# Block-sparse attention and soft MoE: a written task order for the attention stage, sampled values copied by either of two engines, and more early places for weights

## The chip, the cores and the metric

The kernel runs on 1 core of one Trainium2 chip. The metric is the device time of one execution in microseconds (us), as the median of several runs. The engines are TensorE (PE; its weight loads are shown apart as PEld), VectorE (DVE), ScalarE (ACT), GpSimd (POOL) and SyncE (SP), which only issues transfers here. Each engine takes its instructions in order.

## What is computed

Attention over 4 batches of 8 heads, 768 positions and 64 channels, in blocks of 32: a query block sees its neighbours, the first and last block, and three sampled blocks; the first and last query block see everything. Its output goes through a soft mixture of 8 experts with 4 slots each. All in float32.

```python
mask = np.abs(blk_i - blk_j) <= window
mask = mask | (blk_i == 0) | (blk_j == 0) | (blk_i == n_blocks - 1) | (blk_j == n_blocks - 1)
for qb in range(n_blocks):
    for kb in sampled_blocks[qb]:
        mask[qb * block:(qb + 1) * block, kb * block:(kb + 1) * block] = True
scores = np.where(mask, scale * q @ k.T, -1e9)
x = softmax(scores) @ v                      # rows of all heads side by side: 3072 x 512
logits = x @ phi                             # 3072 x 32 slots
slot_input = softmax(logits, axis=0).T @ x
h = np.maximum(slot_input[e] @ w1[e], 0.0)   # for each expert e: 4 x 512 @ 512 x 1024
slot_out[e] = h @ w2[e]
out = softmax(logits, axis=1) @ slot_out
```

## The kernel before

**Stages.** Attention runs for about 250 us, batch by batch (b = 0 to 3). Each batch has two "dense" items (the first and last query block against all keys: scores `sd`, products `avd`) and 11 "pair" items of two query blocks each. Then follows the expert part: first layer (`pf`, 128 matmuls), second layer (`pso`, 256 matmuls), and the combination with the output (`po`, `ob`).

**A pair item.** POOL copies the neighbouring and the two outer key blocks into a staging tile `kst` (`fixed`, L455 and L457); ACT or POOL adds the three sampled ones, whose block numbers stand in registers (`sampled_`, L463 and L465). The registers are filled by loads from the tables `sreg` and `vreg` (`block_numbers`, L362), three numbers a load. The query block is loaded by SP (`load_q`, L330) and scaled by ACT or POOL (L498, L500). PE forms the scores `s` (`qk`, L536: 32 matmul passes of a tile 64 rows by 32 columns). DVE takes the negated maximum `nm` (L551), ACT the exponentials `p` (L556), DVE the 32 x 32 transposes `ptt` (L563). POOL copies the sampled values to `vrs` (`stage_v`, L481, three copies of 128x260 a query block). Then PE multiplies with the values into `av` (`av_heads`, L628), DVE divides by the sums into `x` (L621 to L623), and PE transposes `x` (`mxt`, L823).

**Tilings of TensorE.** `av_heads` writes three widths one after another: the two outer blocks 128 columns wide, two neighbours 64 wide, the rest (other neighbour and the sampled blocks) 32 wide. Scores are 32 wide, transposes use the full 128 x 128 array, logits `ml` and slot sums `ms` 128 rows by 32 columns.

**Groups.** Four `x` tiles make a group: logits `ml`, their running maximum, `md`, `lt` and `ms` (`plan_group`).

**What sets the order.** Every piece of work is a task with a key, dependences, buffers that it takes, and one or more engines with a cost. `Plan.run` is a list scheduler: at each step it starts the task that can start earliest, with the key (shifted by the table `OFF`) deciding among near ones, and picks the engine for tasks with two. It emits the instructions in that order; where PE would stand idle it adds matmuls on the identity (`warm`, L396, tile `st`). Weight loads during attention are "paced": they are tied to a PE instruction of about their planned time.

**Weights.** The two layers are cut into 64 halves of 512 KB. 11 have places of their own, 15 take the room of keys, values and dense probabilities that are done with, 15 (`LORD`) the room of the attention's staging tiles when that stage ends; the other 23 wait for a half that has been used (`done_w`, `next_w`). All are issued by SP at L231.

Of the kernel before, what the change touches and what calls it, by code (L numbers as in the profile page):

```python
# [57 lines left out]
LORD = [0, 1, 2, 3, 4, 5, -1, -2, -3, -4, 6, 7, 8, -5, -6]  # L58
LCOLS = [slice(c, c + LC) for c in range(0, WP, LC)]
# [3 lines left out]
SWITCH = 0.095  # L63
BACK = {"PE": 0.17, "DVE": -0.07, "ACT": -0.1, "POOL": -0.06, "SP": 0.0, "NONE": 0.0}
OFF = {"acc": 4.15, "av": 2.35, "av1": 4.1, "av2": -5, "avo": -4.9, "avo1": -5, "ce": 5, "cm": -2.05,
       "cn": 0.65, "dav": 3.7, "davo": -3.85, "dexp": 1.8, "do": 2.9, "dqk": 0.05, "dt": 4.55, "dtop": 0.85,
       "dtrn": -4.55, "exp": 2.7, "fix": 4.3, "ldq": 3.55, "lexp": -1.45, "lg": -0.55, "lo": -2.85, "lp": -5,
       "lt": 5, "ltop": -5, "qk": 0.85, "scl": 3.05, "smp": 3.9, "sum": -3.1, "top": -4.8, "trn": 0.2,
       "vst": 4.7, "xt": -2.8, "xto": -1}
# [5 lines left out]
class Task:  # L75
    def __init__(self, f, opts, deps, key, acq, byte, pre, pace, kind, mode, ni):
        self.pace, self.kind, self.mode, self.ni = pace, kind, mode, ni
        self.f, self.opts, self.deps, self.key = f, opts, [d for d in deps if d], key
        self.acq, self.byte, self.pre = list(acq), byte, pre
        self.start = self.fin = self.eng = None  # L80


class Plan:
# [6 lines left out]
    def add(self, f, opts, deps, key, acq=(), byte=0, pre=None, pace=False, kind=None, mode=None, ni=0):  # L90
        t = Task(f, opts if isinstance(opts, list) else [opts], deps, key + OFF.get(kind, 0.0), acq, byte, pre, pace,
                 kind, mode, ni)
        self.tasks.append(t)
        return t

    def run(self):
        tasks = self.tasks
# [3 lines left out]
        left = {t: len(t.deps) for t in tasks}  # L101
        ready = {t: 0.0 for t in tasks}
        out = {t: [] for t in tasks}
        for t in tasks:
            for d in t.deps:
                out[d].append(t)
# [3 lines left out]
        queue = {p: sorted([t for t in tasks if any(q == p for q, _ in t.acq)], key=lambda t: t.key)  # L110
                 for p in self.pools if p not in self.free}
        gives = {t: [] for t in tasks}
        spans, open_ = [], {}
        avail = [t for t in tasks if not t.deps]
        order = []
        while avail:
            cand = []
            for t in avail:
                r, ok, k = ready[t], True, {}
                for p, _ in t.acq:  # L120
                    i = (nxt[p] + k.get(p, 0)) % self.pools[p]
                    k[p] = k.get(p, 0) + 1
                    if (p in queue and queue[p][0] is not t) or held[p][i]:
                        ok = False
                        break
                    r = max(r, slot[p][i])
                if ok:
                    if t.pace:
                        r = max(r, paced)

                    st, e, d = min(((max(r, at[e]), e, d) for e, d in t.opts), key=lambda z: (z[0], z[0] + z[2]))
                    if e == "PE" and t.mode and t.mode[0] != mode:
                        d += SWITCH
                    cand.append((st, t.key, st + d, t, e, d))
            assert cand, [(t.key, t.opts) for t in avail][:8]
            soon = min(c[:3] for c in cand)
            eng = min(cand, key=lambda c: c[:3])[4]
            st, _, en, t, e, d = min((c for c in cand if c[4] == eng and c[0] <= soon[0] + 0.05), key=lambda c: c[1:3])
            avail.remove(t)
            if e == "PE":  # L140
                mode = t.mode[-1] if t.mode else None
            t.start, t.eng, at[e] = st, e, en + BACK[e] + (0.11 if t.kind in ("qk", "dqk") else 0.0)
# [9 lines left out]
            else:  # L152
                t.fin = en
            order.append(t)
            for p in {p for p, _ in t.acq}:
                if p in queue:
                    queue[p].pop(0)
            for p, users in t.acq:
                i = nxt[p]
                nxt[p] = (i + 1) % self.pools[p]  # L160
                held[p][i] = set(users)
                for u in users:
                    gives[u].append((p, i))
                spans.append([p, i, st, 1e9])
                open_[p, i] = spans[-1]
# [5 lines left out]
            for o in out[t]:  # L171
                left[o] -= 1
                ready[o] = max(ready[o], t.fin + LAG[e])
                if not left[o]:
                    avail.append(o)
        assert len(order) == len(tasks), len(tasks) - len(order)

        todo = {e: [t for t in order if t.eng == e and t.pre] for e in at}
        pe_end = 0.0
        pe = []  # L180
        for t in order:
# [4 lines left out]
            if t.eng == "PE":  # L186

                if (t.start > self.fill[0].fin and t.start - pe_end > 0.45
# [15 lines left out]
def attn_moe_kernel(ctx, tc, qT, kT, vfull, vtab, sampled, phi, w1, w2, out):  # L204
# [968 lines left out]
    with tc.manual_schedule(engines={E_.SP}):  # L1173
        plan.run()
# [280 lines left out]
```

## Time and profile before

| | |
|---|---|
| median of 3 runs | 311.37 us (309.15 to 311.98) |
| span of the profiled execution | 305.7 us |
| PE busy | 277.5 us (91%), 7161 matmuls and 7161 weight loads |
| DVE, ACT, POOL busy | 215.4, 166.1, 178.9 us |
| moved by DMA | 63.61 MB, mean 208 GB/s |
| granted clock of PE | 1.00 nearly everywhere (mean 0.984) |

The span runs from the first to the last instruction of the profiled execution; the run times also hold what lies around it. A row of a timeline merges neighbouring instructions of one kind: its second number runs to the end of the last one. Ends of matmuls are modelled, so how long a piece of PE work really took is best read from its start to the start of the next piece. "issue" as the end of an idle time means that the profile shows nothing that was waited for.

### The profile page before, as it was taken

Reading aid. Unit: us, or ns where it says so; the run is one execution under the profiler, and the core shown is the slowest. Engines: PE = TensorE matmul, PEld = TensorE weight load, DVE = VectorE, ACT = ScalarE, POOL = GpSimd, SP = SyncE. Lnnn points to the kernel's source line nnn. Section 1 sums busy time; section 2 is a strip of 40 time slices with the busy share of each in tenths; the row PEclk is TensorE's granted clock in tenths of the full one; section 3 lists DMA queues with packets and bytes.
Section 4 is the critical chain, followed back from the end, with each engine's and each line's share of the span. In section 5 each row is a group of like instructions: output and inputs, shape, how many; then the busy total and the mean of one; then the engine's idle time right before and its main releaser. Section 6 shows DMA issues by size and latency. Waiting matters only on the chain.

```text
span 305.7 us, 17569 instructions
## 1 busy us (share of the span) xinstructions
PE 277.5 (91%) x7161; PEld 193.2 (63%) x7161; DVE 215.4 (70%) x494; ACT 166.1 (54%) x515; POOL 178.9 (59%) x501
## 2 busy tenths in 40 slices
PE   7688999799999999999999999999897999999950
PEld 6248775476687767767777767867665763355640
DVE  4698878458998779988988879998676545012360
ACT  0875847453667877446689654695641142102450
POOL 2669589927855899684599977579753504000000
PEclk9899999999999999999999999999999999999995
DMA  7946677630166672035376320778979998999998
GB/s 238 401 122 174 184 203 219 171 109 3 38 181 186 192 188 78 5 90 142 115 206 192 118 74 21 206 194 232 232 215 317 412 404 286 401 409 407 369 314 274
DMA packets 31634, 63.61 MB, mean 208 GB/s; under 512 B 5313, under 2 KB 18754, under 8 KB 31554
## 3 DMA queue, kind: packets, MB, share of 16 engines
q1 hardware_dynamic: 31408, 62.37, 64.1%
q8 instruction: 56, 0.92, 1.2%
q14 instruction: 24, 0.20, 0.2%
q10 hardware_dynamic: 146, 0.13, 0.1%
HBM read 56.19 MB, written 6.29 MB: 204 GB/s over the span
## 4 chain that ended last, share of the span: by engine, by line
PE 76%; DMA 7%; issue 4%; ACT 3%; DVE 2%; POOL 1%; SPq 1%; POOLq 1%; ACTq 1%
PE av L628 30%; PE s L536 11%; PE avd L628 7%; PE pso L1261 5%; PE pf L1253 5%; PE mxt L823 4%; DMA q<-in_qT_dram 4%; PE sd L732 4%; PE ml L859 2%; DMA v<-in_vfull_dram 2%; PE ms L909 2%; PE po L1357 1%; DMA out_dram<-ob 1%; POOLq L362 1%; PE st L396 1%
## 5 line engine op out<-in xcount | busy, mean ns | idle before, releaser
L481 POOL COPY vrs<-v 128x260 f32 x264 | 94.7, 405 | 25.4 <-PE av L628 17.5
L556 ACT ACTIVATE p<-s,nm 128x256 f32<-128x256 f32 x176 | 72.3, 483 | 13.9 <-DVE nm L551 12.5
L628 PE MATMUL av<-v,ptt 64*64 64x130 f32 (+2 forms) x1728 | 75.8, 285 | 1.4 <-issue 1.3
L628 PEld LDWEIGHTS av<-v,ptt 64*64 64x64 f32 (+2 forms) x1728 | 50.1, 131 | 25.7 <-issue 18.7
L563 DVE STREAM_TRANSPOSE ptt<-p 128x512 f32<-128x512 f32 x88 | 57.3, 688 | 4.5 <-ACT p L556 3.8
L551 DVE TENSOR_REDUCE nm<-s 128x2 f32<-128x512 f32 x88 | 54.9, 680 | 4.0 <-PE s L536 3.8
L536 PE MATMUL s<-kst,q 64*32 64x256 f32 x1408 | 51.9, 385 | 6.4 <-POOL kst L465 3.0
L457 POOL COPY kst<-ktile 128x384 f32<-128x384 f32 x88 | 43.1, 506 | 15.4 <-PE s L536 14.6
L628 PE MATMUL av<-vrs,ptt 64*32 64x130 f32 x2112 | 46.9, 275 | 3.8 <-issue 3.7
L463 ACT ACTIVATE kst<-ktile 128x128 f32 x177 | 40.9, 310 | 11.7 <-PE s L536 10.4
L536 PEld LDWEIGHTS s<-kst,q 64*32 64x32 f32 x1408 | 30.5, 107 | 18.9 <-POOL kst L465 4.9
L628 PEld LDWEIGHTS av<-vrs,ptt 64*32 64x32 f32 x2112 | 35.8, 105 | 6.2 <-issue 5.7
L374 ACT COPY xT<-mxt 128x512 f32<-128x512 f32 (+1 forms) x25 | 14.1, 564 | 32.4 <-PE mxt L823 32.3
L628 PE MATMUL avd<-v,ptd 64*64 64x130 f32 x768 | 22.8, 271 | 1.5 <-DVE x L623 1.4
L628 PEld LDWEIGHTS avd<-v,ptd 64*64 64x64 f32 x768 | 21.6, 132 | 3.2 <-issue 1.6
L465 POOL COPY kst<-ktile 128x128 f32 x87 | 21.8, 293 | 0.5 <-issue 0.5
L621 DVE TENSOR_SCALAR rs<-av 128x8 f32<-128x8 f32 (+2 forms) x28 | 4.3, 155 | 23.7 <-PE av L628 23.7
L500 POOL TENSOR_SCALAR q<-q 128x256 f32<-128x256 f32 x23 | 9.3, 406 | 19.0 <-DMA q<-in_qT_dram 15.7
L732 PE MATMUL sd<-ktile,q 64*32 64x384 f32 x256 | 18.4, 510 | 0.9 <-ACT p L556 0.5
L498 ACT ACTIVATE q<-q 128x256 f32<-128x256 f32 x25 | 10.4, 425 | 15.3 <-DMA q<-in_qT_dram 15.2
L763 ACT ACTIVATE pd<-sd,nb 128x384 f32<-128x384 f32 x32 | 16.6, 580 | 3.5 <-DVE nb L758 3.1
L750 DVE TENSOR_REDUCE nm<-sd 128x1 f32<-128x384 f32 x32 | 16.2, 545 | 2.7 <-PE sd L732 2.7
(122 smaller groups left out, 290.1 us busy)
## 6 DMA issues: line engine op xcount, KB each, us to landing
w<-in_w_dram SPq DMA_DIRECT2D x20, 512.0 KB, 8.7
v<-in_w_dram SPq DMA_DIRECT2D x12, 512.0 KB, 10.5
q<-in_qT_dram SPq DMA_DIRECT2D x47, 128.0 KB, 2.7
w<-in_w_dram SPq DMA_DIRECT2D x44, 128.0 KB, 3.4
out_dram<-ob SPq DMA_DIRECT2D x22, 256.0 KB, 3.3
ktile<-in_kT_dram SPq DMA_DIRECT2D x48, 96.0 KB, 2.9
v<-in_w_dram SPq DMA_DIRECT2D x24, 128.0 KB, 4.4
kw<-in_w_dram SPq DMA_DIRECT2D x6, 512.0 KB, 8.7
```

What stands on the lines that cost most here:

```text
L457: POOL.tensor_copy(out=st[:, :, w:w + 96], in_=kv[:, :, (i - 1) * BLK:(i + 2) * BLK])
L463: ACT.activation(out=st[:, :, o:o + BLK], in_=src, func=AF.Copy, scale=1.0)
L465: POOL.tensor_copy(out=st[:, :, o:o + BLK], in_=src)
L481: POOL.tensor_copy(out=st[:, :, j:j + 1, :], in_=vf[:, :, ds(t.vals[j], 1), :])
L536: PE.matmul(u.s[r][32 * p:32 * p + 32, j, :], lhsT=u.q[s_, p, j, :], rhs=kd[j][0][s_, p, :], start=True, stop=True)
L551: DVE.tensor_reduce(out=u.nm[r], in_=u.s[r], axis=AX.X, op=ALU.max, negate=True)
L556: ACT.activation(out=u.p[r][:, j, :], in_=u.s[r][:, j, :], func=AF.Exp, bias=u.nm[r][:, j:j + 1], scale=1.0)
L563: DVE.transpose(out=T.pt[r][:, :, 2 * w:2 * w + 2, :].rearrange("p k j q -> p j k q"), in_=u.p[r].rearrange("p j (k q) -> p j k q", k=8))
L628: PE.matmul(av[:, r * 2 * D1:(r + 1) * 2 * D1].rearrange("p (a d) -> p a d", a=2), lhsT=lhsT, rhs=rhs, start=start, stop=stop)
L732: PE.matmul(u.s[r][k][32 * p:32 * p + 32, :], lhsT=T.dq.q[s_, p, j, :], rhs=kt[s_, p, 384 * k:384 * (k + 1)], start=True, stop=True)
L750: DVE.tensor_reduce(out=u.nm[r][:, k:k + 1], in_=u.s[r][k], axis=AX.X, op=ALU.max, negate=True)
L763: ACT.activation(out=u.p[r][k], in_=u.s[r][k], func=AF.Exp, bias=u.nb[r], scale=1.0)
```

## The change

1. `OFF`, the keys and the list scheduler no longer set the order: a table `ORDER` of 1291 task numbers does, for all engines; a `+` at a number takes the second engine of that task. The planned times that remain serve the pacing and how far ahead registers are loaded. The idle matmuls of `warm` inside the attention are no longer made.
2. `av_heads` can run its widths upwards (32, 64, 128) when the work ahead left the array 32 wide (`up`).
3. Sampled values may be copied by ACT (`stage_v`). Staging tiles are assigned when the task runs, not when it is planned.
4. Block numbers of the two query blocks of a pair are loaded together, six a load, once for each engine that uses them.
5. Transposes of two `x` tiles form one task.
6. Some two-input DVE operations on 1 or 2 columns become one-input ones (`nb`, `nmx`, `ssum`), and the subtraction and the product of the second softmax move to POOL (`c_low`, `c_share`).
7. Four more weight halves get a place: two in buffers of `ptt` and one in two buffers of `x` (asked for at the scores of the last item but one, `qks[N - 2]`), one in two buffers of `xT`.
8. `pf` takes other PSUM banks, since `pc` and `ph` are made first.

```diff
+ORDER = """
+0 21 4 5 1 6 7 9 8 37 2 14 3 10 16 12 38 13 22 15 11 17 82 23 65 20 29 25 18 24 33 34 35 26 36 63 30 27 78 28 39 79+
...
+""".split()
...
-        while avail:
...
+        for word in ORDER:
+            t = self.tasks[int(word.rstrip("+"))]
+            e, d = t.opts[word.count("+")]
...
             if e == "PE":
+                t.up = t.turn and t.mode[0] != mode and t.mode[-1] == mode
...
-                if (t.start > self.fill[0].fin and t.start - pe_end > 0.45
-                        and sum(p == "s" and a < t.start and z > pe_end for p, _, a, z in spans) < SB):
-                    self.fill[1](int((t.start - pe_end - 0.15) / 0.28))
...
+    def block_numbers(b, t, i, eng, most):
+        j = (i - 1) // 2
+        key = b, most, j, eng
+        if key not in both:
+            _, both[key] = nc.values_load_multi_w_load_instructions(
+                t[0:1, 2 * j + 1:2 * j + 3, :], engines=[{"ACT": E_.Activation, "POOL": E_.Pool}[eng]], min_val=0, max_val=most,
...
             for j in range(NR):
-                POOL.tensor_copy(out=st[:, :, j:j + 1, :], in_=vf[:, :, ds(t.vals[j], 1), :])
+                o, src = st[:, :, j:j + 1, :], vf[:, :, ds(t.vals[j], 1), :]
+                if t.eng == "ACT":
+                    ACT.activation(out=o, in_=src, func=AF.Copy, scale=1.0)
+                else:
+                    POOL.tensor_copy(out=o, in_=src)
...
-        for n in range(NR + 1):
+        for n in ((1, 2, 3, 0) if up else range(NR + 1)):
...
+        todo = low + mid + wide if up else wide + mid + low
...
-                DVE.tensor_tensor(out=u.nb[r], in0=nm[:, 0:1], in1=nm[:, 1:2], op=ALU.min)
+                DVE.tensor_reduce(out=u.nb[r], in_=nm, axis=AX.X, op=ALU.min)
...
+            t_t = add(turns, ("PE", 0.44 if len(both) == 1 else 0.85), sum([z[1].out for z in both], []), n + 2, kind="xt", mode="F", ni=8 * len(both),
+                      acq=[("pt", z[4]) for z in both] + [("xT", z[5]) for z in both])
...
+    for j in range(NPT):
+        add(lambda t, m=m + j: load_w(m, turned), ("SP", 0.47), [qks[N - 2]], N + j / 10, acq=[("ptt", end_use)], byte=4 * WP * P,
+            kind="lw")
...
+    add(lambda t, m=m + NPT: load_halves(m, "x", XB), ("SP", 0.94), [qks[N - 2]], N + 0.2, acq=[("x", end_use)] * 2, byte=4 * WP * P,
+        kind="lx")
...
+    wpool.append(None)
+    load_halves(len(wpool) - 1, "xT", XTB)
...
+    psF.tile([P, 4, P], F32, tag="po", name="pc", bufs=3)
+    ph = psF.tile([P, 8, NS], F32, tag="f1", name="ph", bufs=1)
     pf = [psF.tile([P, 512], F32, tag="pf", name=f"pf{hf}", bufs=2) for hf in range(2)]
```

On PE, in batch 0, around the second pass of transposes before: scores of two pair items, one tile's transposes, and a product with its three widths downwards (the first number of a size is the width in columns; a row stands for so many equal matmuls).

```order
L536 MATMUL s<-kst_95,q_97 32x256 x8
L536 MATMUL s<-kst_96,q_97 32x256 x8
L823 MATMUL mxt<-ident,x 128x128 x4
L628 MATMUL av<-v_68,ptt 128x130 x4
L628 MATMUL av<-v_68,ptt 64x130 x8
L628 MATMUL av<-v_68,ptt 32x130 x8
L628 MATMUL av<-vrs_103,ptt 32x130 x2
```

The end of the product that follows the same scores now, and what comes after it.

```order
L671 MATMUL av<-vrs_102,ptt 32x130 x2
L671 MATMUL av<-vrs_101,ptt 32x130 x2
L671 MATMUL av<-v_68,ptt 32x130 x8
L671 MATMUL av<-v_68,ptt 64x130 x8
L671 MATMUL av<-v_68,ptt 128x130 x4
L882 MATMUL mxt<-ident,x 128x128 x8
L671 MATMUL av<-v_68,ptt 128x130 x4
L671 MATMUL av<-v_68,ptt 64x130 x8
```

The product behind the scores begins 32 wide, as the scores are, and ends 128 wide; two tiles are transposed together, and the next product runs downwards from 128.

Counted over all of PE's rows up to the second layer of transposes for the row sums (`mr`), the array's tiling changes 184 times before and 154 times now; `st` has 24 matmuls before and 13 now.

On ACT, in batch 0, exponentials `p` and sampled keys `kst` before (an `ISA` row computes an address from a register):

```order
L362 TENSOR_LOAD sreg
L556 ACTIVATE p<-s,nm 128x256 x2
L362 TENSOR_LOAD sreg
L463 ISA
L463 ACTIVATE kst_95<-ktile 128x4x32
```

and now, where the loads from `vreg` and the copies to `vrs` stand between them:

```order
L394 TENSOR_LOAD vreg
L599 ACTIVATE p<-s,nm 128x256 x3
L394 TENSOR_LOAD vreg
L522 ISA
L522 ACTIVATE vrs_103<-v_68 128x2x130
```

ACT now holds register loads ahead of its exponentials as before, and the copies of values behind them.

On SP, the last paced weight pieces (32 rows each) and the first late halves (128 rows) before:

```order
L231 DMA v_68<-in_w_dram 32x1024 x14
L231 DMA ptd<-in_w_dram 32x1024 x12
L231 DMA kw<-in_w_dram 128x1024 x3
L231 DMA w_7108<-in_w_dram 128x1024
L231 DMA w_7110<-in_w_dram 128x1024
```

and now:

```order
L258 DMA kw<-in_w_dram 128x1024
L258 DMA w_7241<-in_w_dram 128x1024
L258 DMA w_7244<-in_w_dram 128x1024
L258 DMA kw<-in_w_dram 128x1024
L258 DMA v_68<-in_w_dram 32x1024 x2
L1184 DMA w_7336<-in_w_dram 128x512
L1184 DMA w_7337<-in_w_dram 128x512
L258 DMA w_7608<-in_w_dram 128x1024
```

The three halves in buffers of `ptt` and `x` (`w_7241`, `w_7244`, and `w_7336` with `w_7337`) stand ahead of the first half that takes the room of a staging tile (`w_7608`). Behind the 15 `LORD` halves comes the fourth; 19 halves wait for used ones, before 23.

Over the whole program POOL's copies to `vrs` go from 264 to 168 and ACT's from 0 to 96; sampled keys on POOL from 87 to 150, on ACT from 177 to 114; query scalings on POOL from 23 to 35, on ACT from 25 to 13; `xT` copies on ACT from 23 to 13, on DVE from 0 to 10; register loads on POOL from 117 to 76, on ACT from 59 to 58.

## Rows read from the trace of the kernel before

**Rows 1.** The page: busy time, share and instructions; DMA queue of instructions, packets and MB.
```profile
PE 277.5 (91%) x7161; PEld 193.2 (63%) x7161; DVE 215.4 (70%) x494; ACT 166.1 (54%) x515; POOL 178.9 (59%) x501
...
q8 instruction: 56, 0.92, 1.2%
```

**Rows 2.** Windows: stretch, length, busy us (instructions) by engine, clock, DMA share, GB/s.
```profile
44.00:61.00 17.00, 14.03 (x392) 8.74 (x388) 10.65 (x20) 11.53 (x36) 16.68 (x49) 1.00 0.70 192
61.00:203.00 142.00, 139.06 (x4271) 103.89 (x4276) 123.83 (x272) 93.81 (x300) 104.53 (x296) 1.00 0.43 121
203.00:252.00 49.00, 44.48 (x1129) 32.22 (x1131) 31.86 (x84) 22.33 (x73) 25.77 (x70) 1.00 0.92 296
160.00:170.00 10.00, 10.00 (x370) 7.99 (x372) 8.02 (x17) 7.97 (x26) 9.87 (x29) 1.00 0.67 194
```

**Rows 3.** Timeline of PE, 44 to 61 us: start, length, instructions, idle before.
```profile
45.84 1.33 PE L536 MATMUL s<-kst,q 64*32 64x256 f32 x31
...
49.19 0.66 PE L823 MATMUL mxt<-ident,x 128*128 128x128 f32 x4
49.77 1.71 PE L628 MATMUL av<-v,ptt 64*128 64x130 f32 x40
...
52.13 1.71 PE L628 MATMUL av<-v,ptt 64*128 64x130 f32 x40
...
54.41 0.62 PE L536 MATMUL s<-kst,q 64*32 64x256 f32 x6
...
59.73 0.66 PE L823 MATMUL mxt<-ident,x 128*128 128x128 f32 x4
```

**Rows 4.** Timeline of PE, 83 to 98 us.
```profile
88.52 1.96 PE L536 MATMUL s<-kst,q 64*32 64x256 f32 x64
90.41 0.65 PE L823 MATMUL mxt<-ident,x 128*128 128x128 f32 x4
90.99 1.71 PE L628 MATMUL av<-v,ptt 64*128 64x130 f32 x40
...
93.18 1.51 PE L536 MATMUL s<-kst,q 64*32 64x256 f32 x32
```

**Rows 5.** Timelines of ACT (44 to 61 us) and of SP's issues (30 to 60 us).
```profile
56.56 0.42 ACT L498 ACTIVATE q<-q 128x256 f32<-128x256 f32 x1 [4.03 <-DMA q<-in_qT_dram]
...
45.51 5.79 SPq L354 DMA_DIRECT2D v<-in_vfull_dram  x10
...
52.42 0.35 SPq L330 DMA_DIRECT2D q<-in_qT_dram  x1
```

**Rows 6.** Timeline of PE, 200 to 246 us.
```profile
231.63 0.88 PE L628 MATMUL av<-vrs,ptt 64*32 64x130 f32 x41
234.57 0.42 PE L628 MATMUL av<-vrs,ptt 64*32 64x130 f32 x7 [2.06 <-issue]
```

**Rows 7.** Waits: who waited for what, us in total, times, longest.
```profile
PE av L628 <- issue: 5.0, 7, 2.1
```

**Rows 8.** Instructions of line 362: duration ns min/median/max, first and last start.
```profile
L362 POOLq TENSOR_LOAD <-vreg x88: 721/728/751, 14.8 to 228.8; - x88
L362 ACTq TENSOR_LOAD <-sreg x59: 692/702/889, 2.2 to 219.0; - x59
```

**Rows 9.** Groups by line and shape: busy us, mean ns of one, idle before.
```profile
L481 POOL COPY vrs<-v 128x260 f32 x264 | 94.7, 405 | 25.4 <-PE av L628 17.5 <-PE s L536 2.2 <-DMA q<-in_qT_dram 1.9
...
L498 ACT ACTIVATE q<-q 128x256 f32<-128x256 f32 x25 | 10.4, 425 | 15.3 <-DMA q<-in_qT_dram 15.2
```

**Rows 10.** Late weights: SP's issues, a window, landing on the page, the chain.
```profile
252.83 6.07 SPq L231 DMA_DIRECT2D w<-in_w_dram  x9
...
275.34 1.68 SPq L231 DMA_DIRECT2D w<-in_w_dram  x2
...
252.00:256.00 4.00, 4.00 (x40) 1.30 (x36) 3.70 (x15) 1.21 (x3) 2.28 (x3) 1.00 0.76 232
...
w<-in_w_dram SPq DMA_DIRECT2D x20, 512.0 KB, 8.7
...
287.32 1.86 PE pso L1261 x32
```

More of the change, by code (lines that the diff above doesn't have):

```diff
@@ L62 @@
 HEAD = -4096
[L63 to L69, printed above, removed]
+SWITCH = 0.13
+FETCH, BORDER = 4.05, 192
+BACK = {"PE": 0.03, "DVE": -0.07, "ACT": -0.1, "POOL": -0.06, "SP": 0.0, "NONE": 0.0}
+ORDER = """
[47 rows of a table added]
+""".split()
 E_ = mybir.EngineType
@@ L100, in run @@
         mode = None
[L101 to L104, printed above, removed]
+        count, border, entered = 0, BORDER, -100.0
+        ready = {t: 0.0 for t in self.tasks}
+        out = {t: [] for t in self.tasks}
+        for t in self.tasks:
             for d in t.deps:
@@ new lines, in schedule @@
+        gives = {t: [] for t in self.tasks}
+        spans, open_, order = [], {}, []
+        for word in ORDER:
+            t = self.tasks[int(word.rstrip("+"))]
+            e, d = t.opts[word.count("+")]
+            st = max(ready[t], at[e], paced if t.pace else 0.0)
+            for p, users in t.acq:
+                i = nxt[p]
+                assert not held[p][i]
+                nxt[p] = (i + 1) % self.pools[p]
+                st = max(st, slot[p][i])
+                held[p][i] = set(users)
+                for u in users:
+                    gives[u].append((p, i))
+                open_[p, i] = [p, i, st, 1e9]
+                spans.append(open_[p, i])
+            if e == "PE":
+                t.up = t.turn and t.mode[0] != mode and t.mode[-1] == mode
+                if t.mode and t.mode[-1 if t.up else 0] != mode:
+                    d += SWITCH
+                mode = t.mode[0 if t.up else -1] if t.mode else None
+                n = t.ni + 2
+                while border < count + n:
+                    b = st + d * (border - count) / n
+                    wait = max(0.0, entered + FETCH - b)
+                    d += wait
+                    entered = b + wait
+                    border += 256
+                count += n
+            t.start, t.eng, at[e] = st, e, st + d + BACK[e]
@@ L152, in run @@
             else:
-                t.fin = en
+                t.fin = st + d
             order.append(t)
[L155 to L165, printed above, removed]
             for p, i in gives[t]:
@@ L359, in load_v @@
         return i
-    def block_numbers(t, i, eng, most):
-        _, vals = nc.values_load_multi_w_load_instructions(
-            t[0:1, i, :], engines=[{"ACT": E_.Activation, "POOL": E_.Pool}[eng]], min_val=0, max_val=most,
-            skip_runtime_bounds_check_because="block numbers lie in range by the definition of the input")
-        return vals
+    both = {}
+    def block_numbers(b, t, i, eng, most):
[4 more added lines that the diff above has]
+                t[0:1, 2 * j + 1:2 * j + 3, :], engines=[{"ACT": E_.Activation, "POOL": E_.Pool}[eng]], min_val=0, max_val=most,
+                skip_runtime_bounds_check_because="block numbers lie in range by the definition of the input")
+        o = (i - 2 * j - 1) * NR
+        return both[key][o:o + NR]
     def place(b, t):
@@ L916, in acc @@
                     continue
-                if gi:
+                if gi and o is ssum:
+                    DVE.tensor_scalar(out=o, in0=o, scalar1=st.al, scalar2=i, op0=ALU.mult, op1=ALU.add)
+                elif gi:
                     DVE.scalar_tensor_tensor(out=o, in0=o, scalar=st.al, in1=i, op0=ALU.mult, op1=ALU.add)
@@ L1082, in f_diff @@
     def f_diff(t):
-        fin.row = pw.tile([1, P], F32, tag="x", name="row", bufs=XB)
+        fin.row = phis[0:1].rearrange("p c s -> p (c s)")
         fin.top = pw.tile([1, NS], F32, tag="top", name="top", bufs=1)
@@ L1171, in attn_moe_kernel @@
     ms.__enter__()
-    plan.fill = max(qks.items())[1], lambda n: warm(None, n)
-    with tc.manual_schedule(engines={E_.SP}):
-        plan.run()
+    late = tc.manual_schedule(engines={E_.SP})
+    late.__enter__()
+    plan.run()
     warm(None, 1)
```

254 lines of the change are left out of this document (142 added, 112 removed), and 46 rows, old and new, of the table ORDER.

## Prediction

> **What bounds the kernel now.** I read the page first: PE is busy 277.5 of 305.7 us, and no other engine passes 71% [rows 1]. PE is therefore the engine whose time has to shrink, either because its work becomes less or because it waits less. Next I read PE by windows, to see where it waits. From 44 to 61 us it is idle for 17.00 - 14.03 = 2.97 us, from 61 to 203 us for 2.94 us in 142, from 203 to 252 us for 4.52 us in 49 [rows 2]. Idle time is not all: an instruction that is held also looks long, so I then measured pieces from start to start in PE's timeline. A double piece of scores (64 matmuls) takes 90.41 - 88.52 = 1.89 us, a tile's transposes 90.99 - 90.41 = 0.58, a product of 88 matmuls that is followed by scores 93.18 - 90.99 = 2.19 [rows 4]. Against these prices, the scores at 45.84 take 3.35 us and those at 54.41 take 5.32 [rows 3]: 1.46 + 3.43 = 4.9 us lost, most of what the window shows as idle being in it.
>
> What ended the longer of these two waits? ACT stood for 4.03 us until 56.56, waiting for a query block that it was to scale [rows 5]; its exponentials lay behind, and with them the score buffers that PE needs. That block was issued by SP at 52.42, behind ten value pieces that kept SP for 5.79 us from 45.51 on [rows 5]. At the same time POOL is busy 16.68 of 17.00 us [rows 2]. In the last stretch the longest wait is another: 2.06 us at 234.57, inside a product whose inputs were all there ("issue") [rows 6]; seven such waits of PE sum to 5.0 us [rows 7].
>
> **The change part by part.**
>
> *Fewer tilings.* The array changes its tiling 184 times before and 154 times now, 30 less. A product followed by another product takes 52.13 - 49.77 = 2.36 us [rows 3], and one followed by scores, which stay 32 wide, 2.19 [rows 4]: one change costs 0.17 us. The upward order (32 to 64 to 128) is in no row; the same two borders lie in it, so I charge it the same. 30 x 0.17 = 5.1 us at most, and nothing where PE would have waited anyway (a stretch with gaps swallows it). I take 0.15 a change: **-4.5 us**. The 11 matmuls of `st` that go filled idle time; they cost and gain nothing, since what covered them is the wait itself.
>
> *The stretch from 44 to 61 us.* Lost are 4.9 us. The new order puts 35 of 48 query scalings on POOL, 23 before, so a late block holds ACT's exponentials less often, and POOL is freed of 96 copies to `vrs` at 94.7 / 264 = 0.36 us each [rows 9], 34 us, against 63 more sampled keys, shorter copies of 128 instead of 260 elements, so at most 63 x 0.36 = 23 us. SP still puts runs of value pieces between query blocks. Bounds 0 and 4.9; I take **-3.5**, nearer to the top because both causes are eased.
>
> *61 to 203 us.* Idle are 2.94 us [rows 2], spread over many short waits; bounds 0 and 2.9; half or a little more is what a new order may find: **-2**.
>
> *203 to 252 us.* Idle are 4.52 us [rows 2]. The wait of 2.06 [rows 6] is no wait for data, so reordering moves it rather than removing it. Bounds 0 and 4.5; **-2**.
>
> *Copies on ACT.* A copy of 128x260 on ACT is not in the trace; the nearest is the scaling of 128x256 at 0.425 us [rows 9]. 96 of them make 41 us, less 63 sampled keys, 10 `xT` copies and 12 scalings that leave, so ACT, busy 54%, ends below 65%: it does not become the bound. But its order is fixed, and three copies in a row (1.3 us) ahead of an exponential delay the transposes and the product behind it. Nothing is lost if the exponential's product lies more than 1.3 us off, and 32 x 1.3 = 41 us if each of the 32 groups is on the path. PE's idle in the calm middle, 2% [rows 2], says that most waits have slack; I charge one and a half groups, 2 us.
>
> *Register loads.* Three numbers take 0.702 us on ACT's sequencer and 0.728 on POOL's, whatever lies around [rows 8]. Six numbers are in no row: between 0.7 (the load counts) and 1.4 (each number counts). There are 117 + 59 = 176 loads before and 76 + 58 = 134 now. If the load counts, 42 loads of 0.7 us go, 30 us over two sequencers; if each number counts, 528 numbers become 804 and 276 x 0.24 = 66 us come. Today these run ahead while the engine works off earlier instructions. I take them at no cost, the cover being those earlier copies; without it up to 0.7 us stand before each of ACT's 58. The Trainium skill ("Runtime: NRT & Kernel Launch", Instruction fetch mechanics) speaks against this edit: it gives about 200 ns a register even in bulk. By that, six numbers would take 1.2 us, near my upper end; the trace's 0.70 for three agrees with it, and the sum by it would be that of the slower rival below, as far as the cover fails.
>
> *The rest.* The two-input DVE operations, the second softmax on POOL and the pairs of block copies lie on engines that PE does not wait for: nothing, as long as DVE keeps its gaps (123.83 busy of 142 us in the middle [rows 2]); if these are gone, the ten `xT` copies come on top of it, at most 6 us. Other banks for `pf`: -0.2.
>
> *Weights.* An earlier end of the attention helps only if the weights follow. Late halves are issued back to back; SP waits once until 252.83 for a used half, and the window behind it moves 232 GB/s at a share of 0.76, about 1 us lost [rows 10]. The last two halves leave SP at 275.34 to 277.0, land about 8.7 us later (285.7), and are used near the end of the piece that runs from 287.32 to 289.18: 2 to 3 us of slack [rows 10]. The four new places close the hole (+1 us), and three halves, 1.5 MB, are asked for before the attention ends. The rest of the late loads hang on staging tiles that come free earlier when attention ends earlier. So I charge nothing.
>
> **Sum.** -4.5 - 3.5 - 2 - 2 + 2 - 0.2 = -10.2 us. The profiled span of 305.7 becomes 295.5. The runs' median lies 311.37 - 305.7 = 5.7 us above that span, which I keep: **301 us**. With the terms' own bounds for likely cases, 296 to 305.
>
> **The rivals.**
>
> *Slower: ACT becomes the step that PE waits for.* Place: register loads and value copies between exponentials of one item. Per group 1.3 us of copies and up to 1.4 us of load, 2.7 us. Gains of 12.2 us (the sum without its 2 us of cost) are eaten when 5 of 32 groups stand on the path with their full price; 3 us more, seven groups in all (18.9), make it slower, 311.4 - 12.2 + 18.9 = **318**. For it: ACT is busy 7.97 of 10 us already at 160 to 170 [rows 2]. Against it: its exponentials today share that room with 177 sampled-key copies, 63 of which leave.
>
> *The instruction stream bounds PE.* 2 x 7161 instructions come in 56 blocks [rows 1], 256 each. From 160 to 170 us PE takes 742 instructions, 2.9 blocks, without a gap [rows 2], one in 3.45 us; the 5.0 us of "issue" [rows 7] come where dense products meet a saturated DMA. If the denser order doubles them: 301 + 5.0 = **306**. The Trainium skill (same page and section) calls crossing a block mostly hidden; by it this rival would not exist, and the 2.06 us of [rows 6] disagree.
>
> *The weights cap it.* If paced pieces and staging tiles keep late loads where they are, PE can come forward only by the slack of 2 to 3 us plus the hole's 1: 311.4 - 4 = **307.4**. Against it: SP's order now asks for three halves earlier.
>
> *Waits only move.* DVE is busy 87% in the middle [rows 2]; less work on PE then turns into waits for DVE, and what stays is part of the 3.5 and 0.2: **309**, no difference that can be told.
>
> **How the numbers follow.** 301 has 0.50; the instruction stream 0.14; the cap 0.10; moved waits 0.16; slower 0.10. About 1% (308.3 and 314.5) is what a measurement can tell from no change. Faster: 0.50 + 0.14 + 0.10 = 0.74; within: 0.16; slower: 0.10. The range leaves out the slower rival and half of the outer ends: 295, where 61 to 252 us lose all their idle time, to 311.
>
> **What would show it.** Right: products next to scores of about 2.2 us and double transposes below 1.2; PE's idle from 44 to 61 us below 1.5 us; attention ending (first `pf`) about 10 us earlier; the last `pso` without a wait for weights. Wrong: "issue" before PE above 8 us; idle time of PE released by ACT's `p` or `vrs`; SP's late issues no earlier than before; six-number loads of 1.4 us with gaps of ACT behind them.

## The result and the profile after

The changed kernel takes 313.97 us (median of 20 runs), the kernel before 309.57 (20 runs beside them): a ratio of 1.0115, 95% interval 1.0076 to 1.0154. It is slower by about 1%; 301 us and a range up to 311 were predicted. (Medians here are over all runs, ratios leave disturbed runs out.) The experiments ran on three chips, each beside runs of the kernel before (medians 306.1 to 307.2 us), so they are compared by ratios.

The profiled execution has a span of 312.1 us. Three lines of its page (busy time of each engine; granted clock of PE in 40 slices of the span; the chain that ended last, by engine), which answer to [rows 1]:

```profile
PE 274.1 (88%) x7139; PEld 194.1 (62%) x7139; DVE 215.5 (69%) x494; ACT 177.3 (57%) x526; POOL 168.3 (54%) x490
...
PEclk9859999999999997999999999999997999999976
...
PE 65%; issue 9%; POOL 7%; DVE 5%; SPq 3%; POOLq 3%; DMA 3%; ACT 2%; ACTq 0%; DVEq 0%
```

The last two of them in the page of before:

```profile
PEclk9899999999999999999999999999999999999995
...
PE 76%; DMA 7%; issue 4%; ACT 3%; DVE 2%; POOL 1%; SPq 1%; POOLq 1%; ACTq 1%
```

PE's busy time fell by 3.4 us, yet PE's share of the chain fell from 76 to 65%. "issue" (nothing that the profile shows was waited for), POOL and DVE took its place, and the clock shows dips at the start, near 118 and near 234 us.

The same windows as in [rows 2], and a last one from the start to the first `pf`, where attention ends (columns as there):

```profile
44.00:61.00 17.00, 15.17 (x439) 11.76 (x440) 13.24 (x25) 13.43 (x42) 11.38 (x35) 1.00 0.67 185
61.00:203.00 142.00, 134.69 (x4230) 101.31 (x4228) 121.51 (x271) 96.85 (x297) 97.41 (x285) 0.99 0.43 123
203.00:252.00 49.00, 40.98 (x1121) 29.41 (x1109) 29.89 (x74) 25.47 (x74) 27.02 (x80) 0.97 0.89 268
...
0.00:258.17 258.17, 230.14 (x6667) 170.38 (x6668) 199.78 (x455) 163.97 (x498) 164.00 (x482) 0.97 0.59 176
```

The last window in before:

```profile
0.00:251.74 251.74, 234.62 (x6690) 170.78 (x6690) 199.70 (x453) 153.16 (x488) 175.16 (x495) 0.99 0.59 177
```

The whole loss lies ahead of the first `pf`: 258.17 - 251.74 = 6.4 us; what follows takes 53.9 us in after (312.1 - 258.2) and 54.0 in before. PE is busy 230.14 us there, 4.5 less than before, and idle 28.03, before 17.12: 10.9 more. Part of the busy time is at half clock. Windows over its low stretches in after, and over the only one of before ahead of `pf`:

```profile
12.50:22.75 10.25, 8.23 (x140) 4.62 (x144) 7.61 (x16) 6.74 (x20) 5.16 (x16) 0.50 0.54 196
...
118.40:121.70 3.30, 3.30 (x98) 2.60 (x86) 3.22 (x6) 2.07 (x10) 3.30 (x10) 0.50 0.45 127
234.40:237.70 3.30, 3.30 (x32) 1.67 (x24) 0.93 (x2) 0.00 (x0) 0.00 (x0) 0.50 1.03 335
```
```profile
12.45:15.86 3.41, 3.35 (x48) 1.60 (x46) 2.88 (x6) 3.35 (x14) 1.19 (x3) 0.50 1.02 400
```

PE was busy for 8.23 + 3.30 + 3.30 = 14.8 us at 0.50 in after, for 3.35 in before. If all of that would halve at full clock, PE's work fell from 234.62 - 1.7 = 232.9 us to 230.14 - 7.4 = 222.7, by 10.2 us; 10.9 us of idle time and 5.7 us of clock took it back.

The loss begins in the first 20 us. The windows there in after and then in before:

```profile
0.00:20.00 20.00, 11.98 (x130) 7.26 (x138) 10.77 (x32) 9.16 (x28) 8.61 (x28) 0.81 0.76 275
```
```profile
0.00:20.00 20.00, 14.62 (x208) 8.88 (x208) 12.77 (x37) 9.38 (x30) 9.55 (x30) 0.91 0.81 287
```

PE is idle for 8.02 us there, 5.38 before: 2.6 of the 10.9 us. Where the first low stretch comes from, in PE's timeline of after (start, length, instructions, idle before):

```profile
8.61 0.88 PE L791 MATMUL sd<-ktile,q 64*32 64x384 f32 x16 [1.25 <-DMA ktile<-in_kT_dram]
12.70 2.33 PE L579 MATMUL s<-kst,q 64*32 64x256 f32 x32 [3.21 <-POOL kst L502]
16.85 3.28 PE L791 MATMUL sd<-ktile,q 64*32 64x384 f32 x32 [1.82 <-ACT pd L822]
```

PE waits 3.21 us for the first pair's keys, as before (2.76); then the second dense scores wait 1.82 us for ACT's exponentials of the first ones, where before they had begun beside the pair's scores. After these waits the clock stays low for 10.24 us instead of 3.41.

### The profile page after: what moved, and what is told of

The parts are those of the page before. It is cut to its first block, busy times and chain, and to the rows that moved or that the text cites. A ratio compares the mean times of both kernels' runs of the same rounds, so it can differ in the third digit from the quotient of the medians.

```text
span 312.1 us, 17436 instructions
## 1 busy us (share of the span) xinstructions
PE 274.1 (88%) x7139; PEld 194.1 (62%) x7139; DVE 215.5 (69%) x494; ACT 177.3 (57%) x526; POOL 168.3 (54%) x490
## 4 chain that ended last, share of the span: by engine, by line
PE 65%; issue 9%; POOL 7%; DVE 5%; SPq 3%; POOLq 3%; DMA 3%; ACT 2%; ACTq 0%; DVEq 0%
PE av L671 26%; PE s L579 9%; PE pso L1386 5%; PE pf L1378 5%; PE avd L671 4%; PE sd L791 4%; PE mxt L882 3%; PE po L1480 3%; POOL kst L494 2%; POOLq L394 2%; PE ms L981 2%; POOL vrs L524 2%; SPq L371 2%; DMA ktile<-in_kT_dram 2%; PE ml L930 2%
## 5 line engine op out<-in xcount | busy, mean ns | idle before, releaser
L524 POOL COPY vrs<-v 128x260 f32 x168 | 60.3, 404 | 42.7 <-PE av L671 23.3
L671 PE MATMUL av<-v,ptt 64*64 64x130 f32 (+2 forms) x1728 | 78.7, 289 | 4.7 <-issue 3.3
L671 PEld LDWEIGHTS av<-v,ptt 64*64 64x64 f32 (+2 forms) x1728 | 54.7, 135 | 27.1 <-issue 21.1
L606 DVE STREAM_TRANSPOSE ptt<-p 128x512 f32<-128x512 f32 x88 | 57.5, 688 | 8.6 <-ACT p L599 8.0
L502 POOL COPY kst<-ktile 128x128 f32 x150 | 38.3, 294 | 7.3 <-issue 5.3
L522 ACT ACTIVATE vrs<-v 128x260 f32 x96 | 32.5, 414 | 14.6 <-PE av L671 10.5
L500 ACT ACTIVATE kst<-ktile 128x128 f32 x114 | 26.5, 303 | 17.2 <-PE s L579 13.6
L543 POOL TENSOR_SCALAR q<-q 128x256 f32<-128x256 f32 x35 | 13.7, 404 | 10.8 <-DMA q<-in_qT_dram 9.0
L826 DVE STREAM_TRANSPOSE ptd<-pd 128x384 f32<-128x384 f32 x32 | 16.4, 553 | 2.2 <-ACT pd L822 2.0
L666 DVE TENSOR_TENSOR x<-av,rs 128x512 f32<-128x512 f32 (+2 forms) x28 | 16.9, 604 | 1.0
L791 PE MATMUL sd<-ktile,q 64*32 64x384 f32 x256 | 14.8, 531 | 3.1 <-ACT pd L822 1.8
## 6 DMA issues: line engine op xcount, KB each, us to landing
v<-in_w_dram SPq DMA_DIRECT2D x12, 512.0 KB, 10.2
kw<-in_w_dram SPq DMA_DIRECT2D x6, 512.0 KB, 10.2
```

Source lines behind the costliest of these rows:

```text
L500: ACT.activation(out=st[:, :, o:o + BLK], in_=src, func=AF.Copy, scale=1.0)
L502: POOL.tensor_copy(out=st[:, :, o:o + BLK], in_=src)
L522: ACT.activation(out=o, in_=src, func=AF.Copy, scale=1.0)
L524: POOL.tensor_copy(out=o, in_=src)
L606: DVE.transpose(out=T.pt[r][:, :, 2 * w:2 * w + 2, :].rearrange("p k j q -> p j k q"), in_=u.p[r].rearrange("p j (k q) -> p j k q", k=8))
L666: DVE.tensor_tensor(out=x, in0=a[:, :, :, 0:D], in1=rs[lo:hi].unsqueeze(3).to_broadcast([hi - lo, 2, 2 * n, D]), op=ALU.mult)
```

## The experiments

In their texts A is the long register loads, B the clock and the fill, C the instruction stream.

### Loads of three numbers, and the fill

`a_three` (after with the old loads):

```diff
-                t[0:1, 2 * j + 1:2 * j + 3, :], engines=[...], min_val=0, max_val=most,
+            t[0:1, i, :], engines=[...], min_val=0, max_val=most,
```

> The changed kernel, with block numbers loaded three at a time again (one query block a load). Six numbers take 1.385 us on GpSimd and 1.33 on ScalarE in the trace of after, three took 0.73 and 0.70, so each number counts. Theory A (the long loads hold copies and exponentials back): waits put down to issue on GpSimd (10.1 us before vrs, 5.3 before kst) and ScalarE (6.4 before p, 3.1 before vrs) fall by more than half, idle time of TensorE released by GpSimd's kst falls below 3 us, and the span falls by 2 to 5 us, to 307 to 310. Theory B (fill and clock): within 1 us of after. Theory C (the dense order itself, TensorE's instruction stream): within 1 us of after.

Measured: 307.93 us, 1.002 (0.9974 to 1.0065). Theory A, at its lower end: 0.95% less than after, 2.9 us, and PE's waits for POOL's `kst` fall from 5.1 to 2.7 us. The loads of after by duration (ns, minimum, median, maximum):

```profile
L394 POOLq TENSOR_LOAD <-vreg x40: 1382/1388/1401, 15.6 to 226.5; - x40
...
L394 ACTq TENSOR_LOAD <-vreg x28: 1319/1332/1351, 16.6 to 224.7; - x28
```

Each number counts: twice as many take 1.9 times as long as in [rows 8]. Waits of after, and one of `a_three` (in total, times, longest):

```profile
POOL vrs L524 <- issue: 10.1, 13, 2.6
...
PE av L671 <- issue: 6.6, 9, 1.9
ACT p L599 <- issue: 6.4, 12, 1.0
...
POOL kst L502 <- issue: 5.3, 8, 1.1
```
```profile
POOL vrs L518 <- issue: 1.8, 6, 0.4
```

How such a load reaches PE, in POOL's timeline of after and then in its chain of waits:

```profile
110.34 1.10 POOL L524 COPY vrs<-v 128x260 f32 x3 [0.48 <-issue]
112.16 1.10 POOL L524 COPY vrs<-v 128x260 f32 x3 [0.72 <-issue]
```
```profile
115.43 0.29 POOL kst L502
115.72 0.24 POOLq L394
115.96 0.24 POOL kst L502
116.19 0.34 POOL kst L492
116.54 0.46 POOL kst L494
117.00 0.04 issue
117.04 1.97 PE s L579 x49
```

POOL loses 1.2 us ahead of two groups of copies, is still at work on `kst` when PE has run out, and holds a next load (`POOLq`) in the same row of work; PE stands for 1.95 us until 117.04 and runs at half clock from 118.3. In `a_three` PE has no wait for POOL in this place. From 61 to 203 us PE is busy 138.14 us there, 134.69 in after:

```profile
61.00:203.00 142.00, 138.14 (x4453) 105.18 (x4440) 127.77 (x283) 102.39 (x313) 103.47 (x305) 1.00 0.48 137
```

`b_six` (before with loads of six, the same edit the other way):

> The kernel before, with six block numbers a load. Theory A: loads of 1.33 to 1.39 us; the same total of numbers or nearly so, but in longer pieces ahead of exponentials: 1 to 4 us slower than before, with issue waits of GpSimd and ScalarE above those of before. Theories B and C: within 0.7 us of before.

Measured: 306.65 us, 0.9988 (0.9949 to 1.0027): no cost. In the old order POOL's waits on issue ahead of `vrs` were 4.3 us, and its copies came early enough. By these runs a long load costs where the engine behind it has no lead.

`a_fill` (after, with the rule of before that puts idle matmuls into PE's waits behind the last scores):

```diff
+                if (t.start > self.fill[0].fin and t.start - pe_end > 0.45 ...):
+                    self.fill[1](int((t.start - pe_end - 0.15) / 0.28))
```

> The changed kernel with idle matmuls put back behind the last scores by the rule of before; it places 13 of them, before had 11. Theory B (without them TensorE stands idle, its clock falls, and the end of the attention takes longer): the low clock stretch of 3.41 us at 234 goes, and the stretch from the last scores to the first pf (226.1 to 258.2, 32.1 us in after, 25.4 in before) loses 1.5 to 4 us; median 310 to 312.5. Theory A and C: within 0.7 us of after, since what came late there (instructions, DVE's ptt) still comes late.

Measured: 311.35 us, 1.0123 (1.0048 to 1.0198): worth nothing, and the low stretch at 234 stayed (3.41 us at 235). It placed 12; the 13th is the one that always stands ahead of `pf`.

`b_nofill` (before without its 11 idle matmuls):

> The kernel before, without its 11 idle matmuls behind the last scores. Theory B: 1.5 to 4 us slower than before, with a low clock stretch between 227 and 255. If the fill only covered waits, as the prediction had it (cost nothing): within 0.5 us of before.

Measured: 305.4 us, 0.9988 (0.9949 to 1.0027): they were worth nothing in before either, and the clock did not fall there.

### The clock at the start

`a_three` still did not gain, although its last score matmul began at 218.4 us, before at 227.0. Two windows of it behind them, and the piece "issue" from its chain of waits that stands ahead:

```profile
232.12 3.37 issue
```
```profile
234.30:244.40 10.10, 8.60 (x84) 5.71 (x84) 1.48 (x7) 1.29 (x6) 1.90 (x5) 0.50 1.02 406
248.00:254.70 6.70, 6.70 (x36) 3.85 (x39) 3.68 (x18) 1.68 (x5) 0.80 (x2) 0.50 0.65 246
```

This is the execution of a mean clock of 0.943, as low as any of the 12 (median 0.958). From the last scores to the first `pf` (251.21 us) it takes 32.8 us, before 24.7. PE is idle for 7.2 us of that, in before for 3.1, and is busy for 12.0 us at half clock, which costs at most 6.0. So waits and clock together gave most of the 8.6 us back. I tried to hold the clock. `a_warm` is `a_three` with the fill at the end, and, ahead of the first pair scores and of the second dense scores, 14 and 8 idle matmuls:

```diff
+    def busy(n):
+        w_ = psA.tile([P, 2, 512], F32, tag="av", name="wm", bufs=1)
+        for _ in range(n):
+            PE.matmul(w_[:, 0, 0:P], lhsT=ident, rhs=ident, start=True, stop=True)
...
+            if not warmed:
+                busy(14)
+            if b == 0 and j == 1:
+                busy(8)
```

> The changed kernel with three numbers a load, the idle matmuls behind the last scores, and 14 and 8 more idle matmuls ahead of the first pair scores and of the second dense scores (8.6 to 17 us), where TensorE stands idle for 3.2 and 1.8 us and then runs at half clock for 10.24 us in after and in a_three. Theory B (what the order gains is lost to the clock; mean clock 0.957 in a_three's runs, 0.977 in before's): the low stretch at 12 us shrinks from 10.24 to at most 3.41 us, the stretches behind the last scores (17.07 us in a_three) to at most 7, and the time falls by 3 to 6 us against a_three: 301 to 305. Theory C (instructions come late, the order gains nothing that a clock could give back): within 1.5 us of a_three.

Measured: 300.63 us, 0.9784 (0.9711 to 0.9857), 2.2% faster than before; theory B. The two halves of it apart:

> Three numbers a load and the 22 idle matmuls at the start alone, none behind the last scores; a_warm measured 0.978 of before, a_three 1.002. If the clock at the start decides: the low stretch of 10.24 us at 12 us goes and nothing else changes for the better, 0.985 to 0.99 (5.1 us of half time is at most what the stretch costs). If the fill at the end decides: above 0.995. If each covers its own stretch: 0.988 to 0.995, between the two.

> Three numbers a load and the idle matmuls behind the last scores alone, none at the start. With long loads the same fill was worth nothing (a_fill 1.0123, after 1.0115). If the end's clock decides once the loads are short: 0.985 to 0.992; if the start decides: 0.998 to 1.004.

Measured: `a_start` 303.65 us, 0.9918 (0.9873 to 0.9964); `a_endfill` 308.15 us, 1.0059 (1.0016 to 1.0102). The start alone gives 1.0% against `a_three`, 3.1 us. PE's timeline at the start of `a_start`, and its window there:

```profile
9.13 3.39 PE L551 MATMUL wm<-ident 128*128 128x128 f32 x28
12.45 1.09 PE L581 MATMUL s<-kst,q 64*32 64x256 f32 x32
13.47 2.05 PE L551 MATMUL wm<-ident 128*128 128x128 f32 x16
15.46 2.36 PE L795 MATMUL sd<-ktile,q 64*32 64x384 f32 x32
```
```profile
8.00:24.00 16.00, 15.41 (x308) 10.28 (x312) 12.17 (x30) 13.59 (x41) 12.15 (x35) 1.00 0.70 255
```

The pair's scores take 1.09 us instead of 2.33, the dense ones 2.36 instead of 3.28, and the clock is 1.00 throughout. The end's fill alone is worth nothing; whether it adds to the start's (0.9784 from 6 runs against 0.9918, on different chips) stays open, since two kernels below with both fills measure 0.984.

The 3.1 us are not the start's stretch alone. In the profile of `a_start` the clock is low for only 3.41 us behind the last scores, where `a_three` had 17.07, and PE is 2.4 us ahead at the last scores and 4.1 us at the first `pf`. Nor does the clock carry all of the end: with those 3.41 us the way from the last scores to the first `pf` still takes 31.1 us. The mean clock of the runs rose from 0.958 to 0.970.

`b_start` (before with 14 idle matmuls ahead of its first pair scores):

> The kernel before with 14 idle matmuls ahead of its first pair scores. Its clock is low for 3.41 us there, so at most 1.7 us are to be had: 0.994 to 1.000. If idle matmuls at the start were worth as much to the old order as to the new one (below 0.99), the gain of a_warm would not be that of the written order set free.

Measured: 304.84 us, 0.9944 (0.99 to 0.9988): 1.7 us, the most that its one low stretch could give. The new order had more to win at the start, 10.24 us at half clock against 3.41.

`a_warm6` (after with loads of six as it came, and all the idle matmuls of `a_warm`):

> The changed kernel with six numbers a load, as it came, and all the idle matmuls of a_warm. If loads and clock are two separate losses, which add: 0.9% above a_warm, 0.987 (302.5 us). If the long loads only cost because their waits dropped the clock: within 0.3% of a_warm, below 0.982.

Measured: 308.57 us, 1.0092 (1.0046 to 1.0139): neither theory. With long loads all the idle matmuls bring 0.3% (1.0092 against 1.0115 and 1.0123, within the intervals), with short ones 2.4% (0.9784 against 1.002, on different chips) or, by `a_start` on the same chip, 1.0%. The mean clock of its runs is 0.979 (0.955 in after, 0.978 in before), so the clock came back and the time did not. This suggests that the losses hide each other: while POOL is late, a faster PE only waits longer, 2.29 and 2.22 us ahead of scores at 101.7 and 115.1 us in its trace, both released by POOL's `kst`.

### The instruction stream

`a_thin` and `b_thin`:

```diff
-                load_w(m, pool, None, slice(0, P), c)
+                load_w(m, pool, None, slice(0, 32), c)
...
+        if m in thin:
+            return ident[:, 0:1].to_broadcast([P, 512 if n < 2 * NE else CW])
```

> The changed kernel with three numbers a load, where the late weight halves bring 32 of their 128 rows and the expert part reads a constant in their place; read up to the first pf only. It tells whether waits put down to issue (3.37 us at 235 in a_three, inside a product of 176 matmuls, at a DMA share of 0.95) come from transfers that share the DMA engines. Theory C1 (the instruction stream is held back by the weights' transfers): in the last 40 us of the attention waits on issue above 0.5 us go, and the stretch from the last scores to the first pf falls from 32.8 us to 27 or less. Theory C2 (the stream is as late without them, since 352 instructions come in a run): the waits stay above 1.5 us in all.

> The kernel before with the same thin late weights, read up to the first pf only. Theory C1: its wait of 2.06 us at 234 goes, and the attention ends 2 to 3 us earlier than in before (first pf at 249 to 250 us). Theory C2: the wait stays. Beside a_thin it gives the gain of the written order without the weights' transfers: 7 to 9 us if the order is worth what the last scores of a_three show (218.4 against 227.0 us), below 3 if the gain is given back behind them.

Measured: `a_thin` 306.03 us, 0.9999 (0.9946 to 1.0051); `b_thin` 307.66 us, 1.0054 (0.9999 to 1.011). The product that stood for 3.37 us in `a_three`, in `a_thin`:

```profile
235.20 0.31 PE L670 MATMUL av<-vrs,ptt 64*32 64x130 f32 x4 [0.41 <-issue]
```

The wait of 2.06 us of [rows 6] is gone in `b_thin` too; one of 1.18 us stands two products later. The waits went as theory C1 has it, the time did not: the first `pf` comes at 247.84 and 249.92 us, before at 251.21 and 251.74; from the last scores to it `a_thin` takes 28.9 us, not 27 or less; and the runs are no faster.

What such a wait is, the packets of the instruction queue in the traces tell, 16 KiB each. In `a_three` PE stands from 232.12 us; a packet starts at 233.1, takes 1.1 us, and PE goes on at 235.49; in before one starts at 231.9 and PE goes on at 234.57; in `a_thin` one starts at 232.3 and PE goes on at 235.20. By these times PE waited for a block of instructions. In `a_three` the packet took no longer than others (median 1.0 us in the first 195 us), but started when PE had already stood for 1.0 us. That the weights' transfers make such packets late is not shown. Kernels with all their weights differ as much among themselves: `b_nofill` has no wait on issue above 0.26 us behind 215 us and its first `pf` at 249.50, as early as `b_thin`; in `a_warm` the longest there is 1.05 us, in `a_start` 3.50. And in `a_thin` PE ran at half clock from 231.0 to 234.4 us, which leaves less of a wait for the same instructions.

### Tilings, copies, the late query block

`a_noup` (`a_three` with all products downwards; 177 changes of tiling instead of 154) and `a_warm_noup` (the same of `a_warm`):

```diff
-                t.up = t.turn and t.mode[0] != mode and t.mode[-1] == mode
+                t.up = False
```

> The changed kernel with three numbers a load and all products running their widths downwards (128, 64, 32), so that the array changes its tiling more often. By the prediction's price of 0.17 us a change, each product that ran upwards costs 0.17 us more where a change of tiling comes back: some 20 to 25 places, 3 to 4 us slower than a_three. If the changes lie in time that TensorE would have waited anyway: within 1 us of a_three.

> a_warm with all products downwards. If a saved change of tiling is worth 0.17 us wherever it is: 3 to 4 us slower than a_warm, 0.988 to 0.992. If TensorE's time is set by other engines' deliveries in most places: within 1 us of a_warm, 0.975 to 0.982.

Measured: 305.26 us, 0.9964 (0.9921 to 1.0007), and 302.74 us, 0.9845 (0.9797 to 0.9892). Against their counterparts (1.002 and 0.9784) the signs differ and the intervals overlap: 23 changes, priced at 3.9 us (1.3%), cannot be seen in the time. The first pair rules such a price out; the second, a difference of 0.6% give or take 0.9, does not. Both pairs ran on different chips.

`a_warm_pool` (`a_warm` with all copies to `vrs` on POOL; the order is not made anew for it):

```diff
-            e, d = t.opts[word.count("+")]
+            e, d = t.opts[0 if t.kind == "vst" else word.count("+")]
```

> a_warm with all 264 copies to vrs on GpSimd (0.405 us each), whose busy time goes from 168 to 207 us of 300. By the prediction the copies on ScalarE cost 2 us: up to 2 us faster than a_warm, 0.972 to 0.978. If GpSimd is then the engine that delivers late: 3 us or more slower, above 0.988, with TensorE's idle time released by its vrs or kst above 10 us (1.5 us and less in a_warm).

Measured: 315.49 us, 1.0218 (1.0149 to 1.0287): 4.4% slower than `a_warm`, and 3.8% slower than the two other kernels with both fills, `a_warm_noup` and `a_warm_q`, on its own chip. Who waits for whom in its profile (an execution of 316.21 us):

```profile
PEld av L680 <- POOL vrs L525: 11.7, 26, 3.3
...
PE s L588 <- POOL kst L503: 8.1, 4, 3.0
```

POOL is the engine that delivers late then. This order needs its copies on ACT. What they gain over an order laid out for copies on POOL is not shown, since `ORDER` stayed as it was. Nor is what the 63 sampled keys cost that moved to POOL: no run puts them back.

`a_warm_q` (`a_warm` with seven of thirteen value pieces behind two query blocks, in SP's order):

```diff
 L364 DMA q_97<-in_qT_dram 128x256
-L388 DMA v_69<-in_vfull_dram 32x910 x11
-L388 DMA v_69<-in_vfull_dram 32x520 x2
+L388 DMA v_69<-in_vfull_dram 32x910 x6
 L364 DMA q_98<-in_qT_dram 128x256
 L364 DMA q_99<-in_qT_dram 128x256
+L388 DMA v_69<-in_vfull_dram 32x910 x5
+L388 DMA v_69<-in_vfull_dram 32x520 x2
```

> a_warm with two query blocks issued by SP ahead of seven of the thirteen value pieces that kept it for 8.27 us from 44.45. If the late block decides in this stretch: it is issued by 49 us, before 52.8, the wait of 2.85 us at 57.5 goes and with it the low clock from 56.7 to 63.5; 3 to 5 us faster, 0.961 to 0.970. If the wait only moves (to the products, whose values then come late, or to GpSimd's kst): within 1 us of a_warm.

Measured: 301.56 us, 0.984 (0.9788 to 0.9892): the wait moved. The block was issued at 50.5 instead of 52.8 us and the wait at 57.5 went, but PE stood earlier, and what it waited for goes back to the query block before that one (POOL's timeline, then PE's, in an execution of 305.02 us):

```profile
47.67 0.40 POOL L544 TENSOR_SCALAR q<-q 128x256 f32<-128x256 f32 x1 [3.49 <-DMA q<-in_qT_dram]
```
```profile
50.18 1.31 PE L680 MATMUL av<-vrs,ptt 64*32 64x130 f32 x36 [3.31 <-POOL vrs L525]
```

POOL holds for a block to scale, its copies to `vrs` stand behind, and PE waits for these.

## Why the prediction was wrong

**Fewer tilings, -4.5 us.** The pieces became as cheap as said. PE's timeline of after:

```profile
214.37 1.71 PE L671 MATMUL av<-v,ptt 64*128 64x130 f32 x40
215.87 0.93 PE L671 MATMUL av<-vrs,ptt 64*32 64x130 f32 x47
216.54 0.37 PE L579 MATMUL s<-kst,q 64*32 64x256 f32 x1
...
219.19 1.09 PE L882 MATMUL mxt<-ident,x 128*128 128x128 f32 x8
220.21 1.71 PE L671 MATMUL av<-v,ptt 64*128 64x130 f32 x40
```

A product next to scores takes 216.54 - 214.37 = 2.17 us, a double transpose 220.21 - 219.19 = 1.02. But `a_noup` and `a_warm_noup` show no time for 23 of the 30 changes. The step that failed is to take a price read from PE's rows for a price of the span. That waits swallow it is likely (PE is idle 10.9 us more) but not shown, as PE still makes 65% of the chain; the double transposes were not tested apart.

**Stretch 44 to 61 us, -3.5.** PE's idle time fell from 2.97 to 1.83 us, above the 1.5 named as the sign. The step that failed is the cause: it was in part misread, and it was not eased. The scores that stood at 54.41 us were held last by POOL, not by ACT, as PE's timeline of before says:

```profile
58.39 1.41 PE L536 MATMUL s<-kst,q 64*32 64x256 f32 x32 [2.08 <-POOL vrs L481]
```

In the chain of before, POOL's copies to `vrs` and 2.7 us of its register loads stand ahead of these scores. And SP still puts thirteen value pieces, 8.80 us, ahead of two query blocks, where [rows 5] had ten and 5.79:

```profile
47.00 8.80 SPq L381 DMA_DIRECT2D v<-in_vfull_dram  x13
```

With more scalings on POOL the late block now holds POOL's copies themselves, as `a_warm_q` shows; in after PE waits 1.07 us for them at 51.84.

**61 to 203 and 203 to 252 us, -2 each.** The idle time rose, from 2.94 to 142 - 134.69 = 7.31 us and from 4.52 to 8.02. Of the first, 3.45 us go with loads of three.

**Copies on ACT, +2.** No run shows this cost; `a_warm_pool` speaks for the other sign, in an order made for copies on ACT. I priced what they add to ACT and left out that POOL delivers to PE, although I had read POOL busy 16.68 of 17 us.

**Register loads, 0.** The first main error. Both bounds stood there, 0.7 and 1.4 us; the upper one holds (1.33 and 1.39). The cover I named, earlier copies, is not there in the new order: 2.9 us by `a_three` against after. With idle matmuls at the start the loads cost more: 1.7% by `a_warm6` against `a_start` (which lacks the fill at the end) on one chip, 3.1% against `a_warm` on another. `b_six` shows no cost in the old order, so the cover was there on the whole. The Trainium skill ("Runtime: NRT & Kernel Launch", Instruction fetch mechanics) gives about 200 ns a register even in bulk; the trace agrees, with 0.22 to 0.24 us a number.

**The clock: no term at all.** The second main error. The sum took the granted clock of before, 1.00 nearly everywhere, for a property of the kernel. The new order makes PE wait 1.82 us for the second dense scores right behind the first wait, and 10.24 us at half clock follow; `a_start` against `a_three` puts 3.1 us on the idle matmuls that hold it. The stretch from 0 to 44 us had no term in the sum either. Together with the loads, after to `a_start`, 1.0115 to 0.9918, 6.1 us are accounted for. Between the 10.2 us forecast as gained and the 3.6 measured as lost lie 13.8; no run accounts for the other 7.7.

**The removed idle matmuls, 0.** Right: `b_nofill`, `a_fill` and `a_endfill`.

**The weights, 0.** Right. The last half is issued at 278.76 us, lands about 8.5 us later and is used at 295.00; no wait for weights stands ahead of `pso`:

```profile
278.76 0.33 SPq L258 DMA_DIRECT2D w<-in_w_dram  x1
```
```profile
295.00 0.61 PE L1386 MATMUL pso<-w,hT 128*32 128x256 f32 x8
```

**The rivals.** The slower one, with a chance of 0.10, had the sign. Its mechanism was half right: loads and copies ahead of exponentials, where the loads cost, the copies show no cost, and it is POOL more than ACT that PE waits for. "issue" ahead of PE's matmuls of `av` rose from 5.0 to 6.6 us; summed over all of PE's matmuls it rose from 6.9 to 10.5, above the 8 named as a sign. So the rival of the instruction stream is not ruled out: blocks of instructions come late, and what makes them late stays open.

**What the forecast had right** is that the order can gain, less than said: `a_warm` reaches 0.9784 from 6 runs, a gain of 6.7 us on the 309.57 of before, where 10.2 were forecast; the two other kernels with both fills gain 1.6%. The order is worth 1.6 to 2.2%, but only with loads of three and idle matmuls that hold the clock. Open stays how much of it the fill at the end carries, and what the upward widths bring.

## What to carry to other kernels

A saving on the busiest engine counts only as far as the engines that feed it deliver earlier too; price every edit at the engine that delivers, by what stands behind it in that engine's order. Two losses may hide each other, as loads and clock seem to here, so undoing one may show almost nothing: undo them together before calling either harmless. A new order changes where the busiest engine idles, and with it the clock it is granted; idle matmuls in a wait at the start were worth 1% here, and behind the last scores alone nothing.

## What the runs showed of the hardware

Register loads take 0.70 us for three numbers and 1.33 for six on ACT, 0.73 and 1.39 on POOL (medians). Waits of 3.21 and 1.82 us, with 32 score matmuls between them, were followed by 10.24 us at half clock (1.2 of 2.4 GHz). A wait of 3.37 us in `a_three` came with 10.24 us too, one of 3.50 in `a_start` with only 3.41, one of 1.95 in after with 3.41, and the waits of 2.06 and 2.08 in before with none. PE's longest wait on issue behind the last scores ended 1.3 to 1.5 us after the end of an instruction packet of 16 KiB (in before, after, `a_three`, `a_start` and `b_thin`).
